# Gated mix of an S4 convolution and a dense block, with all gradients: dense blocks, a weights' load, a transform stage and staging buffers put elsewhere

## The chip, the cores and the metric

The kernel is one program on one core of a Trainium2 chip. TensorE multiplies matrices into PSUM; VectorE (DVE), ScalarE (ACT) and GpSimd (POOL) work on the tensors between; data moves by DMA, issued in this kernel on the queues of SyncE (SP), ScalarE and GpSimd. Every engine works through its own instructions strictly in order, so an instruction that waits holds up all that is queued behind it on that engine. The metric is the device time of one execution in microseconds, and its median over several executions.

## The reference

The sequence u has L = 2048 rows of D = 448 channels. One branch is a state space layer (S4) with N = 256 complex states for each channel, the other a dense block with a squared relu and F = 1792 hidden units. A gate for each row mixes them.

```python
dt = exp(log_dt)[:, None]
logdA = dt * (A_re + 1j * A_im)
P = exp(logdA[:, :, None] * arange(L))
K = einsum("dn,dnl,dn->dl", Cc, P, dt * Bc).real
y = irfft(rfft(pad(u)) * rfft(pad(K)))[:L]      # bfloat16
a = y + u * Dskip
h = x @ w1 + b1;  h = relu(h) ** 2
b = h @ w2 + b2
g = sigmoid((x * gate_w).sum(-1, keepdims=True))
out = g * a + (1 - g) * b                        # x is u
```

Computed are `out` and, for a given `grad_out`, the gradients of u, of the seven S4 parameter tensors, of Dskip, of w1, b1, w2, b2 and of gate_w (14 in all).

## The kernel before

**The S4 branch.** The convolutions go through a transform of length 4096 in two matrix stages. `fwd1` (L221) does the first stage and spills it to a DRAM scratch `gd`; `load_s1` (L247) reads it back turned; `fwd2` (L251) does the second with 16 matmuls a quarter (L259), whose results ScalarE (L208) and VectorE (L209) copy out of PSUM. A spectrum is kept in four quarters, q = 0 to 3. `cmul` (L263) multiplies two of them on VectorE in six operations (L271 to L276). `inv1` (L302) is the first inverse stage: 16 matmuls (L314), copies into a staging tile `st`, and a store to the scratch `hd` issued from ScalarE (L318). `load_hs` (L320) reads `hd` back and `inv2` (L326) is the second inverse stage (matmuls L331 and L333). `inv1` takes its staging tiles in turn: two of the tag `st`, and after them those in the list `K.st_more`, if it isn't empty.

**The order in time.** Up to 180 us: transforms of u and of the gradient signal, the powers of the states (`powers`), and the products for the gradient of the impulse response. Then "DK": `hss`, four tiles read back from `hd` (L718, L719), are multiplied with sum matrices (L991 to L994) into six PSUM banks, copied (L996 to L999), stored to a scratch `dk_d` and read back in another layout, by DMAs put on SP and GpSimd in turn (L1006 to L1016).

Next is the loop over c = 0 to 15 (L1025), in which fourteen or fifteen chunks of 32 channels are done in two half steps. `build_y` (L818, operations L774 to L777) and the x tables grow powers on VectorE; `tables_t` (L857, transposes L866) and `turn_yt` (L870, transposes L878) turn them on TensorE; `kgen` (L830, matmuls L840) makes the impulse response K of the chunk; `dk_chunk` (L889) copies the chunk's DK twice on ScalarE (L891, L892); `back_z` (L894) multiplies it with the tables (128 matmuls L909 for each pair of groups, Z, copied by ScalarE at L913); `back_p` (L922) multiplies Z with the x tables on VectorE (L935) and sums on TensorE (L944). One iteration does the back part of chunk c - 1 and the front part of chunk c.

**The dense branch** is put in as filler. `hidden(lb, jp, banks, ring)` (L597) does two blocks of 128 hidden units for 512 rows: six matmuls with three quarters of the 448 channels (L608), two with the rest (L611), relu on ScalarE (L613), square on ScalarE (L615), a store by GpSimd (L619). jp runs 0 to 6 for each lb = 0 to 3. Six of the seven for lb = 0 are issued at the end of iteration 0 (L1073 to L1075) and use the PSUM banks `NT[4:6]`, which are "S" and "X". After them come `project` (L1079), the transposes of the weights, and `row_block` (L1142 to L1168), the backward dense pass, whose VectorE operation L1164 waits for ScalarE's L1157.

The weights w1 go to a tile `w1v` of the tag `U16`, which earlier holds `Pct` (products for the gradient of K); they are read by three DMAs on SP (L723, L726), issued behind the last load of `hss` (L720 to L726).

**The end.** From 594 us the K rows go through `fwd1`; from 673 us `fwd2` (L1362 to L1366) runs interleaved with `product(0, q, sx[q])` (L1288), which is `cmul` with a spectrum read from `sp_d` and `inv1`; then `product(1, q, ...)` for the gradient of u, q = 0 and 1 here (after `K.st_more = []`), 2 and 3 among the conv outputs. `gradrows` (L1215) reads two rows' blocks of the dense scratch from GpSimd (L1227), turns them by 16 transposes (L1232), copies or squares them on ScalarE (L1233) and multiplies (16 matmuls L1238); 14 of these for w2 (`grad_w2`, L1241) and 14 for w1 (`grad_w1`, L1247) fill TensorE. Conv outputs come next (L1416 and on for `out`, L1460 and on for the gradient of u), then small reductions and the rest of `grad_w1`.

**What sets the order.** The program is written through a scheduler that fixes an order for each engine before the run, from the order in the program, the buffers and the banks. `tc.issue_after(x)` adds one constraint: the instructions inside come after x. A tile of a tag shares its place with other tiles of that tag, so that a write waits for the last reader of what was there.

Of the kernel before, what the change touches and what calls it, by code (L numbers as in the profile page):

```python
# [19 lines left out]
P = 128  # L20
L, D, N, F = 2048, 448, 256, 1792
LT = L // P
FT = F // P
DT = 4
# [314 lines left out]
def kernel(ctx, tc, A_u, A_A_re, A_A_im, A_B_re, A_B_im, A_C_re, A_C_im, A_log_dt, A_Dskip,  # L339
# [3 lines left out]
    nc = tc.nc  # L343
    V, S, G_, T_ = nc.vector, nc.scalar, nc.gpsimd, nc.tensor
# [26 lines left out]
    K = Ker(tc, pool, psum)  # L371
# [61 lines left out]
    ident = const.tile([P, P], bf16, name="ident")  # L433
# [46 lines left out]
    NT = ["N0", "N1", "N2", "N3", "X", "S"]  # L480
# [20 lines left out]
    for nm in nat:  # L501
        r = carve(2 * D).rearrange("p (h d) -> p h d", h=2)
        raw[nm] = r
        ps = K.ps(NT[4 + nti % 2], [P, 2, D], bf16)
# [7 lines left out]
    ps = K.ps("X", [P, FT + 4], bf16)  # L512
# [43 lines left out]
    th, s, q_ = Lr_, dsa[:, 0:2 * D], dsa[:, 2 * D:4 * D]  # L556
# [26 lines left out]
    ps = K.ps("S", [P, 512])  # L583
# [10 lines left out]
    def hsq(j):  # L594
        return SB[:, 4096 + 512 * j:4608 + 512 * j] if j < 13 else w2v[:, 6272:6784]

    def hidden(lb, jp, banks, ring):  # L597
        nonlocal nti, rxi
        ub = UTb[lb % 2]
        rx = ring[rxi % len(ring)]  # L600
        rxi += 1
        pss = []
        for j in (2 * jp, 2 * jp + 1):
            ps = K.ps(banks[nti % len(banks)], [P, 512])
            nti += 1
            pss.append(ps)
            for dt in range(DT - 1):
                T_.matmul(ps[:], lhsT=w1w[:, dt, j * P:j * P + P], rhs=ub[:, dt], start=(dt == 0), stop=False, skip_group_check=True)  # L608
        for k in range(2):
            h, j = slice(64 * k, 64 * k + 64), 2 * jp + k  # L610
            T_.matmul(pss[k][:], lhsT=w1w[h, 3, j * P:j * P + P], rhs=ub[h, 3], start=False, stop=True, tile_position=(64 * k, 0), skip_group_check=True)  # L611
        for k in range(2):
            S.activation(rx[:, 512 * k:512 * k + 512], pss[k][:], ACT.Relu, bias=b1_f[:, 2 * jp + k:2 * jp + k + 1])  # L613
        if jp < 6:
            S.activation(SB[:, 4096 + 1024 * jp:5120 + 1024 * jp], rx, ACT.Square)  # L615
        else:
            for k in range(2):
                S.activation(hsq(12 + k), rx[:, 512 * k:512 * k + 512], ACT.Square)
        G_.dma_start(bass.AP(tensor=rT_d, offset=2 * jp * P * L + 512 * lb, ap=[[L, P], [P * L, 2], [1, 512]]), rx.rearrange("p (k l) -> p k l", k=2))  # L619
# [97 lines left out]
    hss = [b[:, 3584 * i:3584 * i + 3584].rearrange("p (g x d) -> p g x d", g=4, x=2) for b in (hsD, hsP) for i in range(2)]  # L717
    for q in range(4):  # L718
        lhs = K.load_hs(hd[0], q, hss[q], True)  # L719
    w1v = K.t("U16", [P, 8192])  # L720
    w1w = w1v[:, 0:7168].rearrange("p (a f) -> p a f", a=DT)
    with tc.issue_after(lhs.ins):
        nc.sync.dma_start(w1w[:, 0:3], bass.AP(tensor=B_w1.tensor, offset=B_w1.offset, ap=[[F, P], [P * F, 3], [1, F]]))  # L723
    for h in range(2):
        with tc.issue_after(lhs.ins):
            nc.sync.dma_start(w1w[64 * h:64 * h + 64, 3], bass.AP(tensor=B_w1.tensor, offset=B_w1.offset + 384 * F, ap=[[F, 64], [1, F]]))  # L726
    KB = K.t("K28", [P, 14336])
    DK = KB[:, 0:VA * D].rearrange("p (a d) -> p a d", d=D)
    G_.memset(KB[:, 12 * D:VA * D].bitcast(fp32), 0.0)
# [164 lines left out]
    def back_z(c, YTs, gs, kps=None):  # L894

        nonlocal zi
        cc = c % GC
        DKc = DKs[:, c % 2]
        zb = Zr[zi % 2].rearrange("p (s t g n) -> p s t g n", t=2, s=2, g=2)
        zi += 1  # L900
        for gg, g in enumerate(gs):
            psz = K.psF()
            for s in range(2):
                for par in (1, 0):
                    for ii in range(4):
                        i = 2 * ii + par
                        m = (1 + par) * NA
                        for t in range(2):
                            lastz = T_.matmul(psz[32 * ii:32 * ii + m, t, 256 * s:256 * s + 256],  # L909
                                      lhsT=DKc[64 * t:64 * t + 64, s, g, 2 * ii:2 * ii + 1 + par].rearrange("p i a -> p (i a)"),  # L910
                                      rhs=YTs[g][64 * t:64 * t + 64, :, i, :], start=True, stop=True, tile_position=(64 * t, 32 * ii),
                                      skip_group_check=True)
            S.copy(zb[:, :, :, gg].rearrange("p s t n -> p t s n"), psz[:].rearrange("p t (s n) -> p t s n", s=2))  # L913
            if kps is not None:
                with tc.issue_after(lastz.ins):
                    if c % 2 == 0:
                        kgen(c, kps, 2 * g, 2 * g + 2)
                    elif g < 2:
                        kgen(c, kps, 4 * g, 4 * g + 4)
        return zb  # L920
# [62 lines left out]
    ay = x_pair(0, ay)  # L983
    psS = [K.ps(NT[i], [P, 512]) for i in range(4)]
    psE = K.psF()
    tiles = [psS[0], psS[1], psS[2], psS[3], psE[:, 0], psE[:, 1]]
    first, last = {}, {}
    for k, (x8, g, e, gr) in enumerate(ekeys):
# [1 line left out]
        last[e, gr] = k  # L990
    for k, (x8, g, e, gr) in enumerate(ekeys):  # L991
        lt = ct["Ew"][:, 32 * k:32 * k + 32] if k < 128 else Ew2[:, 32 * k - 4096:32 * k - 4064]
        T_.matmul(tiles[e][32 * gr:32 * gr + 32, 0:D], lhsT=lt, rhs=hss[x8 // 2][:, g, x8 % 2, :], start=(k == first[e, gr]), stop=(k == last[e, gr]),
                  tile_position=(0, 32 * gr), skip_group_check=True)  # L994
    stA, stB = (K.t("st", [P, 4, D], bufs=2) for i in range(2))
    for i in range(4):  # L996
        S.copy(stA[:, i], psS[i][:, 0:D])
# [27 lines left out]
    for c in range(NCH + 1):  # L1025
# [7 lines left out]
        if c > 0:  # L1033
            kps = K.ps("X", [P, 16 * NA]) if 1 < c < NCH else None
            z01 = back_z(c - 1, YTs[c - 1], (0, 1), kps)
            if kps is not None and c % 2 == 0:
                k_out(c - 1, kps)
            z23 = back_z(c - 1, YTs[c - 1], (2, 3), kps)
            if kps is not None and c % 2 == 1:
                k_out(c - 1, kps)  # L1040
# [30 lines left out]
                ap = x_pair(c, ap)  # L1071
                x_next(c)
        if c == 0:  # L1073
            for jp in range(6):
                hidden(0, jp, NT[4:6], ring)  # L1075

    ni = 0

# [96 lines left out]
    for (p0, p1) in ((64, 128), (32, 64), (16, 32), (0, 16)):  # L1175
        offs = vp[p0] - LT * p0
        assert all((vp[p] - LT * p == offs).all() for p in range(p0, p1))
        j = 0
# [36 lines left out]
    def gradrows(w, j, nb):  # L1215
# [12 lines left out]
        for th in range(1 if late else 2):  # L1228
            ps = K.ps(nb[ni % len(nb)], [P, 8, P], bf16)
            ni += 1  # L1230
            for tt in range(8):
                T_.transpose(ps[:, tt, :], raw_[:, (8 * th + tt) * P:(8 * th + tt + 1) * P], ident[:])  # L1232
            S.activation(hh[:, 8 * th:8 * th + 8, :], ps[:], ACT.Square if w == 0 else ACT.Copy)  # L1233
        ps = K.ps(nb[ni % len(nb)], [P, 512])
        ni += 1
# [43 lines left out]
    def spk(q):  # L1279
        return s1k[:, q].rearrange("p (a r) d -> p a r d", r=2)  # L1280
# [7 lines left out]
    def product(w, q, sx):  # L1288
        K.cmul(Pk[:, q % 2], sx, spk(q), w == 1, Fc[:, 0:8 * D])
        K.inv1(Pk[:, q % 2], q, hd[1 + w])  # L1290
# [72 lines left out]
    for q in range(4):  # L1363
        K.act_only = False
        if q < 3:
            K.fwd2(s1k[:, q + 1], q + 1, spk(q + 1))  # L1366
        K.act_only = True
        product(0, q, sx[q])
        if q == 0:
            sx.append(load_sx(0, 3))  # L1370
    K.st_more = []
    M8 = K.t("M8", [P, 4096])

    def load_hs(w, q):
# [9 lines left out]
    hsn = load_hs(1, 0)  # L1384
    for q in range(2):
        product(1, q, sx[q])


    for j in range(FT):
# [143 lines left out]
```

## Time and profile before

| | us |
|---|---|
| median of 13 executions | 925.87 |
| lowest, highest | 914.74, 931.62 |
| the profiled execution | 918.52 |
| its span | 916.3 |
| mean granted TensorE clock in it | 0.822 |

The profile is of one execution; all durations come from it. The page's second part cuts the span in 40 slices of 22.9 us, with the busy tenths of each engine:

```profile
PE   1876745737886988798899789989859969988895
DVE  4675857596389998999995999933307968759200
ACT  2887758627977968888877857653515645654543
POOL 2241010113212112121202212333213013354220
PEclk8767566568978797999956789999887779998998
DMA  9797675897543556537656476468998989789762
```

The slices 11 to 22 (229 to 504 us) are the chunk loop's main part: VectorE stands at 9 there. In slices 27 to 30 VectorE has little to do (K's rows and the dense backward pass); slices 30 to 33 hold K's second stage and its products; from slice 34 (756 us) TensorE is nearly full, and in the last two VectorE has nothing.

A line of a timeline reads: start in us, busy us, engine, line and operation, what it writes and reads with shapes, how many were merged, and in square brackets how long the engine stood idle before, with what it waited for.

### The profile page before, as it was taken

The page shows a single profiled execution, that of the slowest core. Times are in us where ns is not written, and L with a number is a line of the kernel's source. Part 1 is how long each engine was busy: PE and PEld are TensorE (multiplying, and loading weights), DVE is VectorE, ACT ScalarE, POOL GpSimd, SP SyncE. Part 2 cuts the span into 40 slices and gives each one's busy share as a digit, 9 for nine tenths or more (in the row PEclk, how much of TensorE's full clock was granted, in tenths as well). Part 3 has the DMA queues.
Part 4 walks back from the last instruction along what each step waited for, and adds up shares of the span by engine and source line. Part 5 has one row for each costly group of instructions (what it writes and reads, how often), then busy time and mean ns, then how long its engine had stood idle before and what let it go on. Part 6 is the DMA issues. An engine that isn't in the chain of part 4 may idle for free.

```text
span 916.3 us, 18876 instructions
## 1 busy us (share of the span) xinstructions
PE 719.3 (78%) x7602; PEld 346.1 (38%) x7633; DVE 639.1 (70%) x1034; ACT 593.8 (65%) x939; POOL 203.2 (22%) x352
## 2 busy tenths in 40 slices
PE   1876745737886988798899789989859969988895
PEld 0432222224343434354455444544223325543353
DVE  4675857596389998999995999933307968759200
ACT  2887758627977968888877857653515645654543
POOL 2241010113212112121202212333213013354220
PEclk8767566568978797999956789999887779998998
DMA  9797675897543556537656476468998989789762
GB/s 229 197 319 262 233 287 221 317 316 200 145 99 93 133 132 137 142 79 142 180 117 132 121 172 152 152 147 281 295 410 243 319 259 260 227 244 273 186 158 63
DMA packets 168238, 184.96 MB, mean 202 GB/s; under 512 B 95347, under 2 KB 145944, under 8 KB 167352
## 3 DMA queue, kind: packets, MB, share of 16 engines
q1 hardware_dynamic: 119062, 83.32, 36.7%
q0 software_dynamic: 21568, 67.46, 22.1%
q10 hardware_dynamic: 27522, 33.00, 11.3%
q8 instruction: 59, 0.97, 0.5%
q14 instruction: 27, 0.22, 0.1%
HBM read 89.60 MB, written 73.13 MB: 178 GB/s over the span
## 4 chain that ended last, share of the span: by engine, by line
PE 31%; ACT 21%; DMA 18%; issue 14%; DVE 11%; POOL 2%; ACTq 1%; SPq 1%; POOLq 0%; DVEq 0%
PE psF L1238 4%; DMA R<-Y 3%; PE psN L1089 3%; PE psX L840 2%; DMA P<-hd 2%; ACT R L913 2%; ACT M L879 2%; PE psN L1238 2%; DMA hd<-st 2%; DMA S<-rT_d 2%; DMA rec_d<-F 1%; PE psN L296 1%; PE psN L608 1%; PE psF L909 1%; DVE F L775 1%
## 5 line engine op out<-in xcount | busy, mean ns | idle before, releaser
L913 ACT CAST R<-psF 128x1024 bf16<-128x1024 f32 x56 | 57.2, 1022 | 30.9 <-PE psF L909 26.3
L935 DVE TENSOR_TENSOR P<-R 128x2048 bf16<-128x2048 bf16 x42 | 49.7, 1218 | 23.0 <-ACT R L913 21.4
L1238 PEld LDWEIGHTS <-S 128*128 128x128 bf16 x448 | 42.0, 101 | 53.2 <-issue 12.8
L1238 PE MATMUL psF<-U,S 128*128 128x448 bf16 x224 | 51.8, 377 | 2.8 <-ACT S L1233 2.8
L909 PE MATMUL psF<-R,S 64*32 64x256 bf16 (+1 forms) x1344 | 35.5, 299 | 18.8 <-DMA R<-Y 9.5
L1089 PE MATMUL psN<-D,S 128*128 128x448 bf16 x208 | 50.2, 373 | 0.0
L774 DVE TENSOR_TENSOR K<-K,F 128x2048 bf16<-128x2048 bf16 (+3 forms) x42 | 36.3, 865 | 7.8 <-ACT F L809 6.2
L774 DVE TENSOR_TENSOR Y<-Y,F 128x2048 bf16<-128x2048 bf16 (+3 forms) x42 | 36.3, 865 | 6.8 <-ACT F L809 5.6
L608 PE MATMUL psN<-S,U 128*128 128x512 bf16 x116 | 37.9, 423 | 3.9 <-ACT M L613 1.2
L209 DVE CAST K<-psN 128x448 bf16<-128x448 f32 x36 | 21.5, 619 | 27.9 <-PE psN L259 26.1
L775 DVE TENSOR_TENSOR F<-Y,F 128x2048 bf16<-128x2048 bf16 (+3 forms) x42 | 35.9, 855 | 4.9 <-ACT F L811 4.9
L1152 PE MATMUL psN<-S,U 128*128 128x512 bf16 x115 | 35.9, 410 | 3.5 <-ACT D L1157 2.5
L775 DVE TENSOR_TENSOR F<-K,F 128x2048 bf16<-128x2048 bf16 (+3 forms) x42 | 35.9, 855 | 3.8 <-ACT F L811 3.7
L777 DVE TENSOR_TENSOR Y<-Y,F 128x2048 bf16<-128x2048 bf16 (+3 forms) x42 | 36.3, 865 | 1.4
L1165 POOL DMA_DIRECT2D dhT_d<-D x28 | 20.4, 729 | 76.2 <-DVE D L1164 69.7
L909 PEld LDWEIGHTS <-S 64*16 64x16 bf16 (+1 forms) x1792 | 21.8, 91 | 40.8 <-issue 18.7
L777 DVE TENSOR_TENSOR K<-K,F 128x2048 bf16<-128x2048 bf16 (+3 forms) x42 | 36.3, 864 | 1.3
L1089 PE MATMUL psN<-S,D 128*128 128x448 bf16 x168 | 36.1, 356 | 1.1 <-DVE D L1164 1.1
L314 PE MATMUL psN<-P,cb_MI 64*128 64x448 bf16 x128 | 28.7, 402 | 10.5 <-ACT st L208 7.7
L1232 PEld LDWEIGHTS <-S 128*128 128x128 bf16 x376 | 24.9, 102 | 23.7 <-DMA S<-rT_d 11.9
L879 ACT COPY M<-psX 128x1024 bf16<-128x1024 bf16 x27 | 27.4, 1015 | 8.3 <-PE psX L878 7.4
L1157 ACT ACTIVATE D<-psN 128x512 bf16<-128x512 f32 x42 | 23.3, 605 | 14.4 <-PE psN L1155 12.7
(409 smaller groups left out, 1965.9 us busy)
## 6 DMA issues: line engine op xcount, KB each, us to landing
sp<-K ACTq DMA_DIRECT2D x8, 896.0 KB, 3.9
hd<-st ACTq DMA_DIRECT2D x16, 448.0 KB, 4.9
dhT_d<-D POOLq DMA_DIRECT2D x28, 256.0 KB, 4.9
R<-sp SPq DMA_DIRECT2D x8, 896.0 KB, 20.9
S<-rT_d POOLq DMA_DIRECT2D x14, 512.0 KB, 5.7
R<-hd SPq DMA_DIRECT2D x16, 448.0 KB, 8.1
rT_d<-M POOLq DMA_DIRECT2D x18, 256.0 KB, 4.5
rec_d<-F POOLq DMA_DIRECT2D x2, 1920.0 KB, 10.0
```

Of the source, the lines that this page charges most:

```text
L314: nc.tensor.matmul(ps[kk2][:, 0:D], lhsT=MI[r0:r0 + 64, ri, :], rhs=sp[r0:r0 + 64, 2 * q2 + ii, ri, :], start=(ri == 0), stop=(ri == 1), t ...
L608: T_.matmul(ps[:], lhsT=w1w[:, dt, j * P:j * P + P], rhs=ub[:, dt], start=(dt == 0), stop=False, skip_group_check=True)
L774: V.tensor_tensor(out=hi, in0=lo, in1=bcast_dims(pr, [0, (None, n // 2), 1]), op=ALU.mult)
L775: V.tensor_tensor(out=Vv.rearrange("p (x a q) -> p x a q", x=rows, q=2), in0=lo, in1=bcast_dims(pi, [0, (None, n // 2), 1]), op=ALU.mult)
L777: return V.tensor_tensor(out=T4[:, :, :, n:2 * n], in0=T4[:, :, :, n:2 * n], in1=V4, op=ALU.add)
L879: S.copy(YT[:, h], pt[:])
L909: lastz = T_.matmul(psz[32 * ii:32 * ii + m, t, 256 * s:256 * s + 256], lhsT=DKc[64 * t:64 * t + 64, s, g, 2 * ii:2 * ii + 1 + par].rearra ...
L913: S.copy(zb[:, :, :, gg].rearrange("p s t n -> p t s n"), psz[:].rearrange("p t (s n) -> p t s n", s=2))
L935: lastp = V.tensor_tensor(out=pr.rearrange("p s t g n -> p s t (g n)"), in0=zv, in1=(xb if r == 0 else rev_dim(xb, 2)), op=ALU.mult)
L1089: lastm = T_.matmul(ps[:, 0:D], lhsT=hblk[j][:, P * tt:P * tt + P], rhs=ws[:, j, :], start=(w == 1 and j == 0), stop=(j == FT - 1))
L1152: T_.matmul(ps[:], lhsT=w2Tw[:, jp, dt, j % 2], rhs=dblk[:, dt], start=(dt == 0), stop=False, skip_group_check=True)
L1238: lastm = T_.matmul(ps[:, 0:width], lhsT=hh[:, t, :], rhs=(DB2[:, t, :] if w == 0 else U[:, t, 0:D + 1]), start=(t == 0), stop=(t == LT - 1))
```

## The change

Four edits.

1. `hidden` gets an argument `after`. In iteration 0 three blocks (jp = 0 to 2) are left; jp = 3 to 5 go to iteration 1, use the banks `NT[0:3]`, and come after `z0`, the last matmul of the first `back_z`.
2. The tile of w1 and its three loads are put behind DK's matmuls in the program. One extra matmul of 128 x 64 into the bank "S" reads `Pct`, which has the tag of w1's tile; it comes after the first DK matmul with x8 = 4, and its result isn't used.
3. In `gradrows` the transposes of the first row come after `f2k`, the last matmul of `fwd2` of K's quarter 2.
4. `K.st_more = []` is put behind `product(1, 0)` and `product(1, 1)`, so that these too take four staging tiles in turn.

```diff
-    def hidden(lb, jp, banks, ring):
+    def hidden(lb, jp, banks, ring, after=None):
...
-            for dt in range(DT - 1):
-                T_.matmul(ps[:], lhsT=w1w[:, dt, j * P:j * P + P], rhs=ub[:, dt], start=(dt == 0), stop=False, skip_group_check=True)
+            with tc.issue_after(after.ins) if after is not None else nullcontext():
+                for dt in range(DT - 1):
+                    T_.matmul(ps[:], lhsT=w1w[:, dt, j * P:j * P + P], rhs=ub[:, dt], start=(dt == 0), stop=False, skip_group_check=True)
...
-    w1v = K.t("U16", [P, 8192])
-    w1w = w1v[:, 0:7168].rearrange("p (a f) -> p a f", a=DT)
-    with tc.issue_after(lhs.ins):
-        nc.sync.dma_start(w1w[:, 0:3], bass.AP(tensor=B_w1.tensor, offset=B_w1.offset, ap=[[F, P], [P * F, 3], [1, F]]))
-    for h in range(2):
-        with tc.issue_after(lhs.ins):
-            nc.sync.dma_start(w1w[64 * h:64 * h + 64, 3], bass.AP(tensor=B_w1.tensor, offset=B_w1.offset + 384 * F, ap=[[F, 64], [1, F]]))
...
-                            lastz = T_.matmul(psz[32 * ii:32 * ii + m, t, 256 * s:256 * s + 256],
+                            lastz = K.last_z = T_.matmul(psz[32 * ii:32 * ii + m, t, 256 * s:256 * s + 256],
...
+    psd = K.ps("S", [P, 512])
...
-        T_.matmul(tiles[e][32 * gr:32 * gr + 32, 0:D], lhsT=lt, rhs=hss[x8 // 2][:, g, x8 % 2, :], start=(k == first[e, gr]), stop=(k == last[e, gr]),
+        K.last_dk = T_.matmul(tiles[e][32 * gr:32 * gr + 32, 0:D], lhsT=lt, rhs=hss[x8 // 2][:, g, x8 % 2, :], start=(k == first[e, gr]), stop=(k == last[e, gr]),
                   tile_position=(0, 32 * gr), skip_group_check=True)
+        if x8 == 4 and ekeys[k - 1][0] < 4:
+            with tc.issue_after(K.last_dk.ins):
+                T_.matmul(psd[:, 0:64], lhsT=ident[:], rhs=Pct[:, 0:64], start=True, stop=True)
+    w1v = K.t("U16", [P, 8192])
+    w1w = w1v[:, 0:7168].rearrange("p (a f) -> p a f", a=DT)
+    with tc.issue_after(lhs.ins):
+        nc.sync.dma_start(w1w[:, 0:3], bass.AP(tensor=B_w1.tensor, offset=B_w1.offset, ap=[[F, P], [P * F, 3], [1, F]]))
+    for h in range(2):
+        with tc.issue_after(lhs.ins):
+            nc.sync.dma_start(w1w[64 * h:64 * h + 64, 3], bass.AP(tensor=B_w1.tensor, offset=B_w1.offset + 384 * F, ap=[[F, 64], [1, F]]))
...
+            if c == 1:
+                z0 = K.last_z
...
-            for jp in range(6):
+            for jp in range(3):
                 hidden(0, jp, NT[4:6], ring)
+        if c == 1:
+            for jp in range(3, 6):
+                hidden(0, jp, NT[0:3], ring, z0)
...
-                T_.transpose(ps[:, tt, :], raw_[:, (8 * th + tt) * P:(8 * th + tt + 1) * P], ident[:])
+                with tc.issue_after(f2k.ins) if hi == 1 and w == 0 else nullcontext():
+                    T_.transpose(ps[:, tt, :], raw_[:, (8 * th + tt) * P:(8 * th + tt + 1) * P], ident[:])
...
             K.fwd2(s1k[:, q + 1], q + 1, spk(q + 1))
+            if q == 1:
+                f2k = K.last_f2
         K.act_only = True
         product(0, q, sx[q])
...
-    K.st_more = []
     M8 = K.t("M8", [P, 4096])
...
         product(1, q, sx[q])
+    K.st_more = []
```

## The prediction

> **What bounds the kernel now.** I read the page's busy table and chain first, then the windows by stage, then the waits of each engine, then the timeline around the longest waits.
>
> ```profile
> PE 719.3 (78%) x7602; PEld 346.1 (38%) x7633; DVE 639.1 (70%) x1034; ACT 593.8 (65%) x939; POOL 203.2 (22%) x352
> PE 31%; ACT 21%; DMA 18%; issue 14%; DVE 11%; POOL 2%; ACTq 1%; SPq 1%; POOLq 0%; DVEq 0%
> ```
>
> No engine is at its limit over the span and the chain changes hands, so the limit must be taken from each stage. The columns of the windows are length, busy PE, PEld, DVE, ACT, POOL, granted clock, DMA share, GB/s.
>
> ```profile
> 245.00:494.00 249.00, 210.73 (x3444) 113.21 (x3458) 230.75 (x278) 202.87 (x275) 46.64 (x79) 0.83 0.55 126
> 673.00:757.00 84.00, 60.13 (x313) 22.36 (x310) 56.44 (x80) 41.79 (x79) 14.58 (x28) 0.76 0.94 297
> 760.00:820.00 60.00, 55.84 (x425) 30.98 (x422) 45.35 (x99) 34.50 (x57) 26.26 (x49) 0.99 0.82 237
> 860.00:916.00 56.00, 45.85 (x294) 23.38 (x293) 0.00 (x0) 23.03 (x53) 8.81 (x15) 0.93 0.47 113
> ```
>
> In the chunk loop (245 to 494) VectorE is busy 93% and TensorE has 38 us free: what starts VectorE's work earlier there is kept, and dense blocks put later fall into TensorE's holes. From 760 on TensorE is the busiest; the last 56 us are TensorE alone. Between, 673 to 757 has nobody full (PE 72%, DVE 67%), and DMA at 0.94.
>
> The waits show three holes, all touched by the change:
>
> ```profile
> DVE P L935 <- ACT R L913: 28.3, 3, 14.4
> PE psX L1232 <- DMA S<-rT_d: 11.2, 1, 11.2
> PE psN L314 <- ACT st L208: 7.7, 1, 7.7
> ```
>
> **Part A: early dense blocks and w1's load.** The first hole, on the timeline:
>
> ```profile
> 226.90 1.01 ACT L892 ACTIVATE S<-K,brow 128x416 bf16<-128x416 bf16 x1
> 227.05 0.41 PE L909 MATMUL psF<-R,S 64*32 64x256 bf16 x7 [1.77 <-ACT S L891]
> 228.18 1.44 PE L608 MATMUL psX<-S,U 128*128 128x512 bf16 x3 [0.71 <-ACT R L848]
> 232.31 0.82 PE L608 MATMUL psX<-S,U 128*128 128x512 bf16 x3
> 244.16 1.04 ACT L913 CAST R<-psF 128x1024 bf16<-128x1024 f32 x1
> 245.23 2.36 DVE L935 TENSOR_TENSOR P<-R 128x2048 bf16<-128x2048 bf16 x2 [14.45 <-ACT R L913]
> ```
>
> Z's operand is ready at 227.9 (L892), but the first pair of products (L935) starts at 245.23. In the 16 us between, hidden's matmuls stand among the Z matmuls, and ScalarE, 13.9 of 16 us busy, puts relu and square of those blocks between the Z copies (L913): a call of hidden, two blocks of 128 units, costs ScalarE 2 x 0.69 + 1.05 = 2.4 us.
>
> In the built order of the changed kernel TensorE has there: DK's matmuls, the new 128x64 matmul as the last of them, x tables, one block ahead of `kgen`, five more behind it, and then Z, 32 matmuls, x tables, 32 more (the first pair); jp 3 to 6 follow spread over chunks 1 and 2. On ScalarE only 4 relus and a square precede L891. So fewer blocks stand between L892 and the second L913, but those that do depend on w1, whose load now starts only when DK's matmuls are done (the extra matmul reads its old buffer).
>
> Gain of the load: DK's last operand quarter took 199.9 to 205.8, 5.9 us.
>
> ```profile
> 199.91 0.54 PE L993 MATMUL psN<-P,M 128*32 128x448 bf16 x2 [0.42 <-DMA P<-hd]
> 205.83 0.55 PE L993 MATMUL psN<-P,M 128*32 128x448 bf16 x3 [1.97 <-DMA P<-hd]
> ```
>
> A quarter is 2 x 448 KB, which at the 350 GB/s seen then is 2.6 us; so at most 3.3 us go to others, of which w1 (1.57 MB, issued at 193.9 on SP) is one. By bandwidth alone, w1's 1.57 MB / 0.34 = 4.6 us would come off. The Trainium skill, "DMA: Bandwidth & Descriptors", section on queues, rings and completion order, says that each DMA engine takes turns between queue rows that have work. w1 sits in SP's row behind SP's own halves of those operands, and w2's 1.57 MB in POOL's row goes on taking its turn; so the rule allows less than 4.6 and the trace at most 3.3. I take 2 us (0 to 3.3).
>
> Price: w1 is issued at about 210 (before: 193.9). 4.6 us plus some 2 to 3 us of start and landing (DK's small reloads took 2.6 to 5.6) put it at 217 (215.5 to 220). Behind its three transfers on SP stand the six stores of DK (212.4 to 217.1 before) and the reloads (217.5 to 220.7); one of them must wait until w1 has landed. At 217 this is neutral: DK is read at 226.1 before and at 226 to 228 after. At 220 it costs 3 us. On TensorE, block 1 waits for w1 in front of `kgen` (2.84 us), which then ends near 223, against 223.3 before; five blocks follow.
>
> Here a second rule speaks against the change: "TensorE: Matmul & The Clock Gate", Part 1, has the array at half rate after an idle window of about 3.4 us and full only after as much steady work. The rows above show both rates: three L608 took 1.44 us at 228 and 0.82 at 232. A block is three L608 and an L611: cold 1.44 + 0.6 = 2.0, warm 0.82 + 0.4 = 1.2 us. By the rule, blocks behind the wait for w1 are cold, 5 x 2.0 = 10 us; warm it would be 6. I take one in between, 8 us: blocks done at about 231, Z from 233 to 235 paced by DK's copies (seven L909 took 0.41 us), two L913 copies at 1.0 us with a relu or square between, the first L935 at 239.5 instead of 245.2. Gain 5.5 us; 9 if blocks are warm and DK early, 1 if w1 lands at 220 and blocks are cold.
>
> What of it lives on? The three calls moved into chunk 1 cost TensorE 7 to 12 us and ScalarE 7.2 us, which the loop has room for (ScalarE 203 of 249). The order on every engine is the same again from the ninth `kgen` (463 us before), so the head start arrives there unless TensorE has become the bound. The stretch where it is nearest that:
>
> ```profile
> 463.00:494.00 31.00, 30.63 (x445) 18.31 (x441) 26.43 (x32) 22.34 (x27) 5.90 (x10) 0.50 0.60 107
> ```
>
> TensorE is full there at clock 0.50, which the activity rule alone doesn't explain, but the same work stands there in both, so the shift carries through. I keep 5.5.
>
> **Parts B and C: fwd2(K) ahead of gradient rows, longer staging.** In the order of before, the transposes of the first gradient row (L1232) come after the matmuls of fwd2's q = 0; TensorE waits for the row's load, and VectorE's products wait behind.
>
> ```profile
> 673.87 0.82 PE L259 MATMUL psN<-K,M 128*64 128x448 bf16 x6 [0.24 <-ACT K L208]
> 685.89 0.29 PE L1232 MATMUL psX<-ident,S 128*128 128x128 bf16 x1 [11.20 <-DMA S<-rT_d]
> 693.02 1.08 DVE L271 TENSOR_TENSOR F<-R,K 128x1792 bf16<-128x1792 bf16 x1
> ```
>
> In the changed kernel, 32 fwd2 matmuls (q = 0 and 1) come first, then the 16 of the first inverse (L314), then fwd2's next 14, then the transposes. Nothing is added or removed but order. fwd2's second half, 16 matmuls paced by evacuations of 0.62 us, ends at about 681, and the first complex product can start when its spectrum has landed: of three 896 KB loads, issued from 664.5 with a median of 20.9 us, I put the first at 678.5 (an estimate: two thirds of the median), at worst 686. So product(0,0) starts at 682 rather than 693, 11 us earlier. TensorE doesn't keep all of that: in order behind fwd2 it now waits 6 to 7 us (six operations of 1.08 us) for product(0,0) before the L314, and the gradient rows' 16 transposes and 16 matmuls stand behind. The wait on the row's load gives way to a wait on VectorE. On POOL the row loads follow the transposes, since they have two buffers; a load of them took 5.7 us (median) and has a row's 3 us of matmuls and the next product to land behind, so I cost that at nothing, and at up to 2 us a row if that cover is gone.
>
> The place where both orders meet again is the first conv output (L331, at 757.66 before). Before it stand 72 matmuls L1238 and 88 transposes in the old order, 32 and 48 in the new one. So TensorE owes 40 L1238 (8.2 us, eight took 1.68) and 40 transposes (3 us) more when it gets there: 11 us. I put that L331 at 757.7 - 11 (products earlier) - 7.7 (the staging wait below) - 3 (of the owed work, as much as had no hole to lie in) = 736; with the owed 11 us that is like 747, against 757.7: 10.7 us. The staging's part of it:
>
> ```profile
> 752.33 0.53 ACT L208 CAST st<-psN 128x448 bf16<-128x448 f32 x1 [8.41 <-DMA hd<-st]
> 752.91 2.21 PE L314 MATMUL psN<-P,cb_MI 64*128 64x448 bf16 x8 [7.65 <-ACT st L208]
> ```
>
> The inverse of product(1,0) waits 7.65 us because ScalarE has only two staging tiles and a store must land first. Four tiles take this wait away, unless the stores, at a DMA share of 0.94, then hold up something behind them. For that I take 9 us for B and C together, not 10.7; low end 3 (the staging wait's gain lost), high end 14 (all owed work in holes). From 760 TensorE is 93% busy with the same work at the same place ("I reaches its 128th" with 256 of L1238 done in both), so the shift carries to the end.
>
> **Sum.** 5.5 + 9 = 14.5 us. The profiled execution: 916.3 - 14.5 = 901.8 span, 918.5 - 14.5 = 904. It lies 7.4 below the median of 13 runs; the median becomes 925.9 - 14.5 = 911.
>
> **Rivals.** (1) The named holes are mostly all kept: 14.4 + 11.2 + 7.7 = 33 us, less some 8 us of displaced work: gain 20 to 30, about 900. For it: VectorE 93% and TensorE 93% after the respective holes. Against: displaced work comes back. (2) Half: w1's landing eats A, or TensorE's wait for product(0,0) at 94% DMA eats B; gain 0 to 10, about 919. For it: w1 goes from 193.9 to 210 and is needed at once. (3) Slower, one mechanism: TensorE is in order, and now stands behind the spectrum loads with no gradient rows to fill. If these land late, the first L331 comes at 746 or later instead of 736, and the 40 + 40 gradient matmuls still owed (11 us) go to the tail, where TensorE is alone: L331 at 757 unmoved gives +11 - 5.5 = +5.5, about 931. It decides from a first product later than 690. For it: DMA 0.94 and loads of 20.9 us; against: those loads stand ahead of the gradient row's in issue order. That the change does nothing is excluded by the built orders.
>
> **Chances.** Gain 10 to 20: 0.45; more: 0.13; 0 to 10: 0.27; slower 0.15. A measurement of this kernel can tell about 1%, 9 us. Faster by over 1%: the first two, and a little of the third, 0.60; within 1%: 0.28; slower 0.12. Range: 897 (upper bounds of A and B, 9 + 14, and some of the first rival) to 929 (short of the slower case's centre).
>
> **What would show it.** First L935 at 239 to 240, at most a relu or square between the first L913s: A right; L608 waiting for U<-in_B_w beyond 219, or DK's L891 after 229: A wrong. The wait L1232 on rT_d gone and the first L271 at 682: B right; a wait of L314 on VectorE over 9 us or first L331 after 746: B wrong. The waits of L208 on hd<-st before the first L331 below 2 us: C right. Wrong altogether if the loop from 245 to 613 lengthens by more than the head start.

## The result and the profile after

| | before | changed |
|---|---|---|
| median, us (runs) | 923.71 (48) | 908.54 (11) |
| lowest, highest | 913.11, 937.68 | 899.47, 920.25 |
| span of the profiled execution | 916.3 | 909.1 |

The change makes the kernel faster: ratio 0.9836, 95% interval 0.9803 to 0.987, or 15.2 us by the medians. The prediction had 14.5 us. The ratios, here and below, leave out each kernel's slower executions and the medians keep all of them; for the kernel called C alone below, where one time of 901.96 lies far under the other 21 and narrows what is kept, the median is the steadier figure. The profiled execution of the changed kernel shows only 7.2 us of the gain: it took 911.26, above its kernel's median, and the one of before 918.52, below its own. This matters below, since a stage that differs between two profiles may differ by chance.

The named waits, first of VectorE (chunk loop), then of TensorE (last third), in the waits of the changed kernel (what waited, for what, us in total, times, longest):

```profile
DVE P L929 <- ACT R L907: 26.4, 4, 11.4
PE psN L314 <- DVE P L276: 11.4, 4, 6.3
PE psN L314 <- DVE P L273: 10.6, 1, 10.6
PE psX L1243 <- DMA S<-rT_d: 2.5, 1, 2.5
```

The first hole shrank only from 14.4 to 11.4 us, because VectorE reached it earlier. TensorE's wait of 11.2 us on a gradient row is 2.5, but now it stands in front of the inverse (L314) waiting for VectorE's products, 22 us in all. The wait of 7.7 us for a staging tile is gone.

The first hole on the timeline of the changed kernel (lines are shifted: L929 was L935, L907 was L913, L885 and L886 were L891 and L892, L609 was L608):

```profile
229.00 1.46 PE L609 MATMUL psS<-S,U 128*128 128x512 bf16 x3
230.93 1.46 PE L609 MATMUL psX<-S,U 128*128 128x512 bf16 x3
...
231.62 0.89 ACT L885 COPY S<-K 128x416 bf16<-128x416 bf16 x1
232.41 1.01 ACT L886 ACTIVATE S<-K,brow 128x416 bf16<-128x416 bf16 x1
234.83 1.01 ACT L907 CAST R<-psF 128x1024 bf16<-128x1024 f32 x1
237.57 1.04 ACT L907 CAST R<-psF 128x1024 bf16<-128x1024 f32 x1
238.64 2.36 DVE L929 TENSOR_TENSOR P<-R 128x2048 bf16<-128x2048 bf16 x2 [11.36 <-ACT R L907]
```

The first two Z copies follow each other in 2.7 us (3.0 before) and the first back_p starts at 238.6 (forecast 239.5, before 245.2). The blocks in front are all at half rate here (1.46 us for three L609), and DK's copies stand on ScalarE behind the relus of those blocks. The first of them starts at 231.6, later than the 229 that the prediction had named as a sign against part A.

The start of K's second stage in the same kernel:

```profile
672.88 1.46 PE L259 MATMUL psN<-K,M 128*64 128x448 bf16 x8 [0.24 <-ACT K L208]
681.63 1.09 DVE L271 TENSOR_TENSOR F<-R,K 128x1792 bf16<-128x1792 bf16 x1 [6.63 <-DMA R<-sp]
684.91 0.93 PE L314 MATMUL psN<-P,cb_MI 64*128 64x448 bf16 x4 [10.57 <-DVE P L273]
735.59 0.55 PE L331 MATMUL psN<-R,negI 128*128 128x448 bf16 x1
```

The 32 matmuls of fwd2's first two quarters end at 674, the first product starts at 681.6, the first conv output at 735.6; the forecast had 681, 682 and 736. But some 4 us of that lead is A's (the last Z copy is 4.2 us early), which the forecast had not put into these times, and a wait for the spectrum's landing (6.63 us) now sets the product's start. So the agreement of the last two is in part luck.

### The profile page after: what moved, and what is told of

It is laid out like the page before. It is cut to its first block, busy times and chain, and to the rows that moved or that the text cites. A ratio compares the mean times of both kernels' runs of the same rounds, so it can differ in the third digit from the quotient of the medians.

```text
span 909.1 us, 18870 instructions
## 1 busy us (share of the span) xinstructions
PE 716.3 (79%) x7602; PEld 345.9 (38%) x7634; DVE 641.2 (71%) x1034; ACT 593.7 (65%) x939; POOL 203.8 (22%) x352
## 4 chain that ended last, share of the span: by engine, by line
PE 36%; DMA 21%; ACT 17%; issue 11%; DVE 10%; POOL 2%; ACTq 1%; SPq 1%; POOLq 0%; DVEq 0%
PE psN L1099 6%; DMA R<-sp 3%; DMA R<-K 3%; PE psX L834 3%; PE psF L903 2%; PE psN L1162 2%; DMA R<-Y 2%; PE psN L296 2%; PE psN L1249 2%; PE psF L1249 2%; DMA R<-hd 1%; DMA rec_d<-F 1%; ACT R L907 1%; DMA U<-in_A_u_dram 1%; PE psX L872 1%
## 5 line engine op out<-in xcount | busy, mean ns | idle before, releaser
L907 ACT CAST R<-psF 128x1024 bf16<-128x1024 f32 x56 | 57.0, 1017 | 28.9 <-PE psF L903 21.4
L929 DVE TENSOR_TENSOR P<-R 128x2048 bf16<-128x2048 bf16 x42 | 49.4, 1217 | 19.1 <-ACT R L907 19.1
L1249 PEld LDWEIGHTS <-S 128*128 128x128 bf16 x448 | 42.2, 100 | 51.5 <-issue 9.7
L609 PE MATMUL psN<-S,U 128*128 128x512 bf16 x133 | 45.3, 432 | 8.1 <-ACT U L614 4.0
L903 PE MATMUL psF<-R,S 64*32 64x256 bf16 (+1 forms) x1344 | 36.1, 306 | 18.8 <-DMA R<-K 9.2
L1249 PE MATMUL psF<-U,S 128*128 128x448 bf16 x224 | 48.7, 363 | 2.0 <-ACT S L1244 1.7
L1099 PE MATMUL psN<-D,S 128*128 128x448 bf16 x208 | 48.2, 365 | 0.0
L314 PE MATMUL psN<-P,cb_MI 64*128 64x448 bf16 x128 | 26.7, 411 | 23.4 <-DVE P L276 11.4
L1162 PE MATMUL psN<-S,U 128*128 128x512 bf16 x115 | 37.1, 421 | 4.2 <-ACT D L1167 2.8
L1167 ACT ACTIVATE D<-psN 128x512 bf16<-128x512 f32 x42 | 23.2, 602 | 14.4 <-PE psN L1165 12.7
L938 PE MATMUL psS<-P,cb_sel 128*32 128x256 bf16 x224 | 31.2, 322 | 1.0 <-issue 0.4
L209 DVE CAST K<-psN 128x448 bf16<-128x448 f32 x36 | 21.4, 620 | 14.9 <-PE psN L259 13.9
## 6 DMA issues: line engine op xcount, KB each, us to landing
R<-sp SPq DMA_DIRECT2D x8, 896.0 KB, 22.4
```

The source lines that it names most:

```text
L903: lastz = K.last_z = T_.matmul(psz[32 * ii:32 * ii + m, t, 256 * s:256 * s + 256], lhsT=DKc[64 * t:64 * t + 64, s, g, 2 * ii:2 * ii + 1 + ...
L929: lastp = V.tensor_tensor(out=pr.rearrange("p s t g n -> p s t (g n)"), in0=zv, in1=(xb if r == 0 else rev_dim(xb, 2)), op=ALU.mult)
L938: T_.matmul(sps[s][32 * gr:32 * gr + 32, r, :], lhsT=sel[:, k, off:off + 32], rhs=Q[r][:, s, t, gg, :], start=(g < 2 and cc == 0 and t == ...
L1099: lastm = T_.matmul(ps[:, 0:D], lhsT=hblk[j][:, P * tt:P * tt + P], rhs=ws[:, j, :], start=(w == 1 and j == 0), stop=(j == FT - 1))
L1162: T_.matmul(ps[:], lhsT=w2Tw[:, jp, dt, j % 2], rhs=dblk[:, dt], start=(dt == 0), stop=False, skip_group_check=True)
L1249: lastm = T_.matmul(ps[:, 0:width], lhsT=hh[:, t, :], rhs=(DB2[:, t, :] if w == 0 else U[:, t, 0:D + 1]), start=(t == 0), stop=(t == LT - 1))
```

## The experiments

Each kernel was timed in alternation with the kernel before. Where times of several kernels are compared I go by medians; ratios are to before, with their 95% intervals.

**The parts by themselves.** From the changed kernel, part A (blocks and w1's load), B (order of gradient rows) and C (`st_more`) were undone in turn.

```diff
 # a_only: B and C undone
-                with tc.issue_after(f2k.ins) if hi == 1 and w == 0 else nullcontext():
-                    T_.transpose(ps[:, tt, :], raw_[:, (8 * th + tt) * P:(8 * th + tt + 1) * P], ident[:])
+                T_.transpose(ps[:, tt, :], raw_[:, (8 * th + tt) * P:(8 * th + tt + 1) * P], ident[:])
...
+    K.st_more = []
     M8 = K.t("M8", [P, 4096])
...
         product(1, q, sx[q])
-    K.st_more = []
```

> Part A alone (three calls of hidden moved to iteration 1, w1's load behind DK's matmuls); fwd2, gradient rows and staging as before. Theory (parts add up, as in the prediction): first product of back_p at 239 to 240 us and 5.5 us faster than before, ratio 0.994 (0.990 to 0.998). Rival (the filler gives the head start back in the loop): first back_p as early, but ratio 0.998 or more. Rival (B and C are worth nothing without a share of the whole gain here): ratio 0.987 or less.

> Part B alone: the first gradient row's transposes behind fwd2's quarter 2; blocks, w1's load and staging as before. Theory: first complex product 11 us earlier, but TensorE only swaps an 11 us wait for others of 6 to 7 us, and the staging wait stays: 4 us faster, ratio 0.996 (0.992 to 0.999). Rival (TensorE's idle time is conserved: it is 24 us in 673 to 757 before and 27 us in the same stage after, so the order alone gives nothing): ratio 0.999 to 1.003. Rival (third of the prediction, TensorE in order behind late spectra): ratio 1.004 or more.

> Part C alone: four staging tiles for product(1,0) and product(1,1). Theory: the wait of 7.7 us for a store to land goes and TensorE owes nothing for it: first conv output some 6 us earlier, and 5 us faster, ratio 0.995 (0.991 to 0.998). Rival (the wait returns at once elsewhere, as a wait for the stores' read-back or for VectorE): ratio 0.999 to 1.001.

> B and C without A. Theory: 9 us faster, ratio 0.990 (0.986 to 0.994), first conv output at about 741 us (as after, 5 to 6 us later). Rival (what B brings is given back by 820 us to waits on the read-backs, as the trace of after suggests: its lead of 22 us at the first conv output is 7 us at the end): ratio 0.995 to 0.998. With A's run the two should add up to the 0.984 of the whole change; if they give less together, A and the rest help each other.

| | ratio (95%) | median, runs | before beside it |
|---|---|---|---|
| A alone | 0.9815 (0.9763 to 0.9868) | 903.86, 6 | 922.63 |
| B alone | 1.0005 (0.9973 to 1.0037) | 925.13, 22 | 922.63 |
| C alone | 0.9875 (0.9828 to 0.9923) | 919.03, 22 | 922.63 |
| B and C | 0.997 (0.9937 to 1.0003) | 921.79, 22 | 922.63 |

A alone brings the whole gain and more, 18.8 us where 5.5 were expected. B brings nothing, as its first rival had said; but that rival's reason, that TensorE's idle time is conserved, does not hold, since the traces below show it growing. C brings 3.6 by the median. B and C together bring 0.8, not 9. The sum was right because two terms were wrong in opposite directions.

**The halves of A.** `blocks_only` leaves w1's load at its old place and moves three calls of hidden; `w1_only` moves the load and leaves six calls in iteration 0.

```diff
 # blocks_only, from a_only (w1's tile and its three loads back behind load_hs)
-    psd = K.ps("S", [P, 512])
...
-        if x8 == 4 and ekeys[k - 1][0] < 4:
-            with tc.issue_after(K.last_dk.ins):
-                T_.matmul(psd[:, 0:64], lhsT=ident[:], rhs=Pct[:, 0:64], start=True, stop=True)
...
 # w1_only, from a_only
-            for jp in range(3):
+            for jp in range(6):
                 hidden(0, jp, NT[4:6], ring)
-        if c == 1:
-            for jp in range(3, 6):
-                hidden(0, jp, NT[0:3], ring, z0)
```

> The blocks' part of A alone: three calls of hidden moved to iteration 1; w1's load where it was, B and C not made. A alone came out 17 to 19 us faster, not 5.5. Theory 1 (the gain is in what stands between DK and the first Z, on ScalarE and TensorE): with w1 early nothing waits for it, and the whole gain is here, 15 us or more, ratio 0.984 or less. Theory 2 (the load takes DMA time from DK's operands, and that is the larger part): 4 to 8 us here, ratio 0.991 to 0.996, and the rest in the run with the load alone. Theory 3 (both are needed): under 4 us in each alone.

> The load's part of A alone: w1 behind DK's matmuls; all six calls of hidden in iteration 0, B and C not made. Theory 1: at most 3 us faster (DK's last operands 2 to 3 us earlier), and possibly slower, since six blocks wait for w1 in front of kgen: ratio 0.997 to 1.004. Theory 2: 10 us or more faster, ratio 0.989 or less. Theory 3: under 4 us.

Blocks: 0.9902 (0.9873 to 0.9931), 912.85 against 922.0. Load: 0.993 (0.99 to 0.9961), 913.74 against 922.0. By medians each half is worth 8 to 9 us and they nearly add up to A (17.4 and 18.8), which none of the three theories had said quite so. The load's half was not to be expected from DK's operands: from the last matmul L296 ahead of DK to DK's last matmul the kernels with the early load took 31.0 to 32.7 us (six profiles), those with the late load 30.0 to 32.2 (eight), on the mean 1.4 us less, near the 2 us forecast. And it pays a price that I had put at nothing. GpSimd on the timeline, first of before, then with the late load (`a_blk1`, below):

```profile
213.46 3.17 POOL L1006 DMA_DIRECT2D dk_d<-st  x6
216.77 2.64 POOL L1014 DMA_DIRECT2D K<-dk_d  x5
```

```profile
211.54 3.17 POOL L1011 DMA_DIRECT2D dk_d<-st  x6
220.02 2.65 POOL L1019 DMA_DIRECT2D K<-dk_d  x5 [5.30 <-DMA dk_d<-st]
```

DK's stores of 28 and 56 KB land in 1.8 to 3.1 us before and in 5.8 to 6.8 with w1 under way at the same time, so the reload is issued 8.5 us after the stores instead of 3.3. From DK's last matmul to the landing of its last reload the kernels with the early load take 12.7 to 14.5 us, those with the late one 16.8 to 18.6. Where the load's half gets its 8 us is therefore not in this stage: in the profile of `w1_only` the first back_p is at 244.2, only 1 us early.

**One early call.** If blocks stand in Z's way, fewer should be better.

```diff
-            for jp in range(3):
+            for jp in range(1):
                 hidden(0, jp, NT[4:6], ring)
         if c == 1:
-            for jp in range(3, 6):
+            for jp in range(1, 6):
```

> Part A with one call of hidden in iteration 0 and five in iteration 1 (A has three and three); B and C not made. In the profile of the changed kernel DK's copy (the last operand of Z) stood on ScalarE from 226 to 231.6 us behind relus of five blocks that TensorE did at half rate. Theory (these blocks stand in Z's way): first back_p another 4 us ahead of A's, and 2 to 4 us faster than A alone, ratio 0.979. Rival (the loop is full: what is put off must be done later, with interest): no faster than A alone, ratio 0.982 to 0.988.

Measured: 0.9806 (0.9755 to 0.9858), 901.41 against 922.0; A alone 903.86. The first back_p comes at 236.9, which is no earlier than in the kernels with three early calls (231.9 to 238.6, below): with the relus out of the way the copies of DK wait for DK itself, which the collision above delays (its last reload lands at 228.8, the first copy starts at 229.4). The two kernels' intervals overlap, so the 2.5 us are not established.

**Where A's lead grows.** I followed the Z copies through the loop. In the changed kernel's first profile the lead on before is 6.3 us at the first copy and still 5.9 at the 40th (485 us). In A alone it is 13 at the first (4.3 of them at 190 us already, ahead of anything that was changed) and 24.9 at the 40th. Programs that differ only after 594 us (A alone and the changed kernel) thus part in the loop.

Five profiles have the changed kernel's front part (changed twice, A, and A and C twice), four have that of before (before, B, C, B and C). At 190 us their means lie 0.8 us apart. The first back_p comes at 231.9 to 238.6 us, 236 on the mean, against 245.2 to 247.8, 246 on the mean: a head start of 10 us. It is 12.8 at the 34th Z copy, 18.7 at the 40th and 18.2 at the last, which is about A's whole gain. So 10 us come from the first hole, some 3 from the loop up to the 34th copy, and 6 from the next six copies.

The stage from the 34th to the 40th copy took 48.6 us in before, 46.1 in the changed kernel's first profile and 39.5 in A alone. It holds the transposes of both weight matrices. The windows of before (columns as in the prediction) show TensorE nearly full, at clock 0.76 and then at half rate:

```profile
442.00:478.00 36.00, 33.85 (x448) 19.89 (x439) 34.31 (x43) 28.44 (x39) 6.39 (x12) 0.76 0.58 146
478.00:491.00 13.00, 12.63 (x275) 8.24 (x274) 12.61 (x14) 9.62 (x12) 4.72 (x8) 0.50 0.41 69
```

VectorE is as full as TensorE in these windows (34.31 of 36 and 12.61 of 13 us), so they don't tell which one bounds the stage. The wait that follows does:

```profile
499.78 0.69 DVE L1164 TENSOR_TENSOR D<-D,M 128x1024 bf16<-128x1024 bf16 x1 [8.97 <-ACT D L1157]
```

VectorE works ahead through the stage and then stands for 9 us, until ScalarE has done L1157 on a result of TensorE whose matmuls stand behind the transposes. The page's slice of 481 to 504 us, where VectorE reads 5 and not 9, is this wait. So TensorE bounds the stage and not, as the loop's mean says, VectorE. To test what TensorE's clock does there, ten matmuls whose result isn't used were put ahead of the transposes, in the kernel before.

```diff
+    psw = K.ps(NT[ni % 3], [P, 512])
+    ni += 1
+    with tc.issue_after(lastm_.ins):
+        for k in range(10):
+            T_.matmul(psw[:], lhsT=w1w[:, 0, k * P:k * P + P], rhs=w1w[:, 1, 0:512], start=(k == 0), stop=(k == 9))
     w1T = SB[:, 0:FT * D].rearrange("p (j d) -> p j d", d=D)
```

Here `lastm_` is the last matmul of the last `project(lb, 0, ...)`.

> The kernel before with ten extra 128x512 matmuls (results unused) right ahead of the weights' transposes, at about 463 us, where the profile of before has TensorE full at granted clock 0.50. From its 34th Z copy to its 40th this stage took 48.5 us in before, c_only, bc_only and 46 in the changed kernel, but 39 to 41 in b_only and in four of the kernels with A or a part of it, at clock 1.00. Theory (TensorE bounds this stage, its transposes keep a high clock but don't raise a low one, and the lead of A grows here by the clock's state, not by less work): with the extra work the clock is at 1.00 through the transposes, the stage takes 40 to 43 us, and the time falls by 0 to 5 us, ratio 0.995 to 1.001. Rival (the transposes themselves pull the clock down): the stage stays at 48 us or more, and the kernel is 2 to 4 us slower, ratio 1.002 to 1.005.

Measured 0.992 (0.9889 to 0.9951), 915.06 (22 runs) against 922.74: 7.7 us faster with work added. The timeline of TensorE, first of before and then of this kernel (L1118 there is L1113), and VectorE's wait in it (L1169 is L1164):

```profile
463.34 5.19 PE L1113 MATMUL psN<-ident,U 128*128 128x128 bf16 x34
468.80 2.25 PE L1113 MATMUL psN<-ident,U 128*128 128x128 bf16 x14
```

```profile
463.92 3.33 PE L1110 MATMUL psN<-U 128*128 128x512 bf16 x8 [0.22 <-issue]
467.09 1.27 PE L1118 MATMUL psN<-ident,U 128*128 128x128 bf16 x12
468.51 1.86 PE L1118 MATMUL psN<-ident,U 128*128 128x128 bf16 x17
496.50 0.69 DVE L1169 TENSOR_TENSOR D<-D,M 128x1024 bf16<-128x1024 bf16 x1 [1.64 <-ACT D L1162]
```

A transpose takes 0.15 to 0.16 us before and 0.11 after the extra matmuls. The same stage of this kernel, in windows:

```profile
472.00:483.00 11.00, 10.41 (x314) 7.24 (x321) 10.62 (x16) 10.66 (x14) 2.19 (x4) 1.00 0.44 98
```

The clock is at 1.00 from 466.8 to 487.3 and the six copies take 41.2 us, extra work included. So the transposes don't pull the clock down at once: the rival falls. The theory holds less strictly than it was put. In before, C and the changed kernel's first profile a half clock lasted through the 31 us of them; but in `a_c_blk1` it rose at 461.9 in their midst, with no wide matmul in front, and fell again at 468.7, and in `w1_only` a full clock fell at 478.0 with 8 us of them to go.

Nor are the 7.7 us the clock's alone. The extra matmuls also changed the order that the scheduler built for VectorE, at the very wait above: seven operations (5.3 us) that stand behind the first L1164 in before stand ahead of it here. In the old order VectorE would have reached it at 489.6 and waited about 7 us for L1162, by my estimate from these times, instead of 9. What the clock is worth by itself is shown by one program in two profiles.

**The changed kernel again.**

> The changed kernel once more, for a second profile and more timed runs beside a_c on one chip. Expected: 908 us, ratio 0.982 to 0.987. If the state of the clock in the weights' transposes explains why the first profile showed a lead of only 6 us where A alone shows 20 or more, then this profile, where it has the stage at 39 us, shows a lead of 15 us or more by 500 us.

0.9856 (0.9805 to 0.9908), 908.12 (6 runs). In this second profile the stage has the full clock:

```profile
427.00:466.00 39.00, 34.90 (x667) 22.09 (x667) 38.04 (x49) 36.31 (x50) 7.12 (x13) 1.00 0.63 154
```

It takes 38.2 us, and the lead on before goes from 7.0 us at the first Z copy to 10.3 at the 34th, 20.7 at the 40th and 15.1 at the 55th. So one program shows a lead of 5.9 or of 20.7 at the same place. About half of the difference, 7.9 us, arises in this stage, in the same order on every engine: from its first transpose to its last it has clock 0.51 in one profile and 1.00 in the other, and VectorE's wait behind it is 9.0 and 2.3 us:

```profile
493.92 0.69 DVE L1174 TENSOR_TENSOR D<-D,M 128x1024 bf16<-128x1024 bf16 x1 [8.96 <-ACT D L1167]
479.75 0.69 DVE L1174 TENSOR_TENSOR D<-D,M 128x1024 bf16<-128x1024 bf16 x1 [2.26 <-ACT D L1167]
```

The other 7 us arise ahead of the 34th copy, and where is open. Before and B alone, whose loop is the same, differ in this stage in the same way: 48.6 us with transposes at 0.50, 41.2 with transposes at 1.00.

**What B and C exchange.** For eight profiles, the time from the last Z copy to the first complex product, from there to the first conv output (L331), and from there to the end of the span:

| | to first product | to first L331 | to the end | sum |
|---|---|---|---|---|
| before | 83.2 | 64.6 | 158.7 | 306.5 |
| A | 80.0 | 66.4 | 163.0 | 309.3 |
| B | 77.1 | 65.7 | 163.1 | 305.9 |
| C | 80.0 | 55.2 | 165.2 | 300.3 |
| B and C | 76.4 | 57.4 | 172.7 | 306.6 |
| A and C | 82.2 | 52.8 | 169.0 | 304.0 |
| changed | 76.1 | 54.0 | 173.5 | 303.6 |
| changed, again | 76.5 | 58.6 | 178.4 | 313.5 |

Over all 14 profiles the first product comes 76 to 77 us after the last Z copy with B and 80 to 84 without; the first output follows it after 53 to 59 us with C and 63 to 66 without. Behind it B gives all of that back and C a part: with both it is 173 to 178 us to the end instead of 158 to 164, of which 11 us are gradient matmuls and transposes still owed (an estimate of the prediction). A row alone proves little, since two profiles of the changed kernel differ by 10 us in the sum. The means of all 14 fit the timed runs: the sum is 307.4 without B and C (six profiles), 303.3 with C (four), 305.9 with B (one), 307.9 with both (three).

What B does is seen in TensorE's idle time, from the first fwd2 of K to the first L331: 23 to 24 us without B and C (six profiles), 15 to 18 with C, 29.3 with B, 25 to 27 with both. C takes 7 us of waiting away; B adds some 5 alone and some 9 beside C, although it does fewer gradient rows in this time. In all four profiles with B VectorE waits 5.9 to 7.0 us for the spectrum, and then TensorE waits 9.8 to 11.0 for VectorE.

For C the chain stands on the timeline of C alone:

```profile
745.89 0.37 ACTq L318 DMA_DIRECT2D hd<-X  x1
753.80 0.68 DVE L1436 SCALAR_TENSOR_TENSOR X<-psN,g,R 128x448 bf16<-128x448 f32 x1 [4.68 <-DMA hd<-X]
759.86 0.69 ACT L1474 ACTIVATE recx<-ident,ds 128x128 bf16<-128x128 bf16 x2 [6.50 <-DVE ds L1446]
761.94 5.86 PE L1241 MATMUL psF<-U,S 128*128 128x448 bf16 x16 [5.73 <-ACT S L1236]
```

The two extra staging tiles lie in X, where the conv output is written too. VectorE (L1436) waits until the store from X has landed; ScalarE's L1474 waits for VectorE; the gradient rows' copy (L1236) stands behind L1474; and TensorE waits 5.73 us for it. The wait of 7.7 us that C takes away comes back as one of 5.7. A and C's first profile shows the same chain (VectorE 6.3, ScalarE 9.0, TensorE 6.7 us). In its second profile and in those of the changed kernel the store from X is not what VectorE waits for, so the price of these tiles isn't the same in every execution.

**Without B, and the best of the pieces.** `a_c` is the changed kernel without B's `issue_after` and `f2k`; `a_c_blk1` has also one early call of hidden.

> A and C without B: the changed kernel without the order edit on the gradient rows. C alone was 4 to 5 us faster and B alone not at all. Theory (A and C add up, B costs some 3 to 5 us): 20 to 23 us faster than before, ratio 0.976 to 0.979, and faster than the whole change. Rival (C's gain depends on what collides with it and A's lead moves it): as A alone, ratio 0.981 to 0.984.

> A and C without B, once more and beside the changed kernel. Theory (B costs 3 to 8 us): ratio 0.974 to 0.980, median 4 to 8 us under that of the changed kernel. Rival (the first run's six executions flattered it): within 2 us of the changed kernel.

> A with one call of hidden in iteration 0, and C, without B: the candidate that should beat both kernels. Both single steps gained 2 to 4 us on A alone. Theory (they add up): 897 us, ratio 0.973 to 0.977. Rival (each is within the spread of A): 901 to 904 us, ratio 0.978 to 0.982.

`a_c`: 0.9799 (0.9734 to 0.9864) and, again, 0.9789 (0.9734 to 0.9844); medians 900.11 and 900.94. Over both runs of each, the mean of `a_c` (12 times) is 901.7 and that of the changed kernel (17 times) 908.0: 6.3 us, with 2.6 to 9.8 as the 95% interval from drawing these times again with replacement. B costs the changed kernel about that. `a_c_blk1`: 0.9744 (0.9692 to 0.9796), 897.73 against 922.74, the fastest median of all kernels here. It is faster than the changed kernel; over `a_c` its lead isn't settled (means 899.9 and 901.7).

## Why the prediction came out right, and what in it was wrong

**The total** was right, 14.5 us forecast and 15.2 measured, but not for its reasons, and that is luck: A was forecast at 5.5 and measured at 18.8; B and C at 9 and measured at 0.8, and in A's company B costs 6.

**A up to the first back_p** seemed right by the changed kernel's own profiles: forecast 239.5, and 238.6 and 238.0 there. Over the five profiles with this front part it is too small: 236 on the mean, a head start of 10 us and not 5.5. The blocks were all at half rate in the first profile alone; in the four others the last three blocks ran at full rate (0.81 us for three L609). The prediction had allowed for this with its 9 us. DK's operands (1.4 us, forecast 2) and w1's landing (218.3 and 219.6 us in the changed kernel, forecast 217) were near. Wrong was that a landing at 217 is neutral for DK: its stores take about 4 us longer beside w1, and its round trip 4 us longer.

**A's step that failed** is "the same work stands there in both, so the shift carries through". I had shown the row with TensorE full at clock 0.50 and taken its clock as given. It is the term that varies: the same program passes the transposes at 0.51 or at 1.00, which is 7.9 us of the stage. The list of VectorE's waits in before had the sign of it, L1164 on L1157 with 21.8 us in all and 9.0 at the longest: VectorE doesn't bound the loop there.

**B** failed at "11 us earlier". The first product was 5.6 us earlier on the mean of the profiles above, since the spectrum's landing sets it when fwd2 no longer does. I had put that landing at two thirds of the median, 13.9 us after the issue; it took 20.9 us in before and 22.4 in both profiles of the changed kernel. That 681.6 met the forecast of 682 is A's lead. The wait of L314 on VectorE, forecast at 6 to 7 us, was 10.6, and four more waits of 11.4 us in all came in the later products. The third rival's mechanism, TensorE in order with no gradient rows to fill, is real; its price was covered by A.

**C's** step "four tiles take this wait away" was right and its condition, that the stores hold nothing up behind them, was not met: the tiles are the conv output's own. The built program shows that X is both; I named the risk as DMA share and not as the tile's next writer.

**The signs** that the prediction had named didn't decide. For A the first back_p came as said, and DK's copy, at 231.6, spoke against; for B the first product came as said, and the wait of L314, at 10.6, spoke against; C's came, the wait was gone, and C is worth little. They told where a wait stands and not what it is worth at the end.

**Open** stays where the load's half of A has its 8 us, as its one profile shows 1 us at the first back_p, 8.0 at the 40th Z copy and 2.6 at the end, and whether A makes the full clock in the transposes more frequent. From the first transpose to the last, four profiles without any part of A and without the extra matmuls had 0.50 (before, C), 0.53 (B and C) and 1.00 (B); of nine with a part of A or all of it, six had 1.00, and the others 0.83, 0.62 and 0.51. That fits, but a profile is one execution, and it isn't proof.

## What to carry to other kernels

A head start reaches the end only through stages that its own engine bounds: look for a long wait of that engine behind a stretch in which another one is full, and if that is TensorE at half clock, treat the clock as a variable worth microseconds. A kernel that only adds work can come out in another order; compare the orders before the time is put down to one cause. When more buffers are lent to a stage, ask who writes these next: the wait may only move there. When a load is put off to clear the way for one transfer, list the small round trips that it will then meet.

## What the runs showed of the hardware

A full TensorE does not by itself get a full clock: through 30 us of transposes and small Z matmuls, busy 30.6 of 31, the granted clock stayed at 0.50 in before, while with ten 128x512 matmuls in front it rose to 1.00 3.7 us after the first of them and stayed there for 20.5 us of the same work. The Trainium skill, "TensorE: Matmul & The Clock Gate", Part 1, tells of about 3.4 us of steady work; for these transposes that did not hold, for the wide matmuls it did. In `a_c_blk1` the clock rose only after 13.7 us of this work, with TensorE busy throughout. And one program's profiles can differ by 15 us of lead in mid-run (5.9 and 20.7) while its times spread over 20 us.
